# One pool for all eight PSUM banks, and every head group's output projection held to the step's end

## The chip, the cores and the metric

The kernel runs on one core of a Trainium2 chip. The metric is the device time of one execution in microseconds. A core has a matrix engine (TensorE; the profile calls its matmuls PE and its weight loads PEld), a vector engine (DVE), a scalar engine (ACT), a general engine (POOL) and a queue engine (SP) that here only issues transfers; 16 DMA engines move the data. TensorE writes its results to PSUM, which has eight banks of 2 KB for each of 128 partitions. Everything else is kept in SBUF.

## The reference

The input has 2048 tokens of 640 features. Four blocks follow one another: attention A, mixer B, attention A, mixer B, with the same weights in both layers. Attention runs over segments of 32 tokens, and every segment takes 8 memory rows from the output of the segment before it:

```python
for s in range(n_seg):                       # 64 segments of 32 tokens
    xs = x[:, s * seg_len:(s + 1) * seg_len, :]
    h = jnp.concatenate([mem, xs], axis=1)   # 8 + 32 rows
    q = jnp.einsum('btd,dhe->bhte', h, Wq)   # 32 heads of 192, D = 640
    k = jnp.einsum('btd,dhe->bhte', h, Wk)
    v = jnp.einsum('btd,dhe->bhte', h, Wv)
    p = softmax(where(mask, q @ k^T * scale, -1e9))
    o = p @ v
    o = jnp.einsum('bhte,hed->btd', o, Wo)
    mem = o[:, :M, :]
    outs.append(o[:, M:, :])
...
# mixer: h = gelu(layernorm(x) @ w1); four quarters shifted along the tokens; x1 = x + h @ w2
#        out = x1 + gelu(layernorm(x1) @ w3) @ w4
```

So a segment can't begin before the output projection of all 32 heads of the segment before it is known. Wq, Wk, Wv and Wo have 7.9 MB each in bf16, and don't fit into SBUF together.

## The kernel before

**Steps and lanes.** The two layers run as two lanes, the second `LAG` = 5 segments behind the first. There are 69 attention steps. In 59 of them both lanes are present, and a matmul then carries 80 columns: per lane 32 tokens and 8 memory rows. Every second step a mixer chunk of 64 tokens per lane begins. Its pieces are spread over the next one to two steps: w1 and w2 in the first step (the "heavy" one below, since the vector work of the mixer stands there as well), w3 over the boundary, w4 in the second ("light") step.

**A step.** The 32 heads are taken in 8 groups of 4 (`g` = 0 to 7). For each group the kernel runs the projections k, q and v (tiles `psk`, `psq`, `psv`: 30 matmuls each, 5 row blocks of the weights by 6), turns v over (`psvt`), then scores (`pss`), softmax in place, the transposed probabilities (`pst`), and the product with v (`pso`), which DVE copies to one of the `oT` tiles in SBUF. Then follows the output projection of the group: 30 matmuls (`f8` in `attention_step`, L653), 6 row blocks of Wo by 5, added up over all 8 groups in two PSUM tiles `psy`. After group 7, ACT copies the memory columns of `psy` into the next step's input (`fm`, L691), and DVE copies the rest for the mixer (`fy`, L699). `psy` is held from the first output matmul of the step until these copies.

**Weights.** SBUF keeps three of the five row blocks of every group of Wk, Wq and Wv, and two (group 0) or four (others) of six of Wo (`CUT`). The rest is loaded again in every step: 48 blocks of 192 KB for k, q, v and 18 blocks of 160 KB for Wo (four for group 0, two for each other group). They go through a ring of 16 slots (`wst`), of which the attention may hold 14 (`RING_A`). SP issues these loads in one queue ("wa"), sorted by due time; a load waits until its slot was read. The mixer's weights use up to five slots and are issued by POOL.

**The order.** `Plan` lists all operations with an engine, a duration and a due time, and `place()` simulates the engines: it takes the operation that can start first, and among those that can start within 0.03 us on TensorE the one with the earliest due time. An operation that needs a PSUM tile can only start when its pool has a free bank and its class is under its limit. The order found is written out; each engine then works through its list in order. `STEP` = 48 is the planned length of a step, `sl` = 6 that of a group.

**Banks.** `PSUM_BANKS` names the pools and `PSUM_USES` gives each class of tile its pool and its limit. The classes are y (the two `psy`), P (projections and `psvt`), S (`pss`, `pst`, `pso`) and B (everything of the mixer). Before, y has two banks of its own, and P, S and B share six, with limits of 4, 3 and 2.

**When an output projection runs.** This is set by `held`, which depends on the number of `oT` tiles:

```python
held = g >= NG - OT_BUFS + 1
at = base + STEP - HOLD + 0.5 * g if held else s0 + 1.9 * sl
ws = [block(t, "o", g, c, at + 0.03 * c) for c in range(GC)]
due = base + STEP - 1 + 0.02 * g if held else s0 + 2.0 * sl
```

With `OT_BUFS` = 7 the groups 2 to 7 are held: their matmuls are due at 47 us of the step, and their Wo blocks at 45 us and later. Groups 0 and 1 have their matmuls due at 12 and 18 us and their blocks at 11.4 and 17.4 us. A first operation on `psy` needs both of its banks at once.

Of the kernel before, what the change touches and what calls it, by code (L numbers as in the profile page):

```python
# [33 lines left out]
W4 = (1.5, 0.025)  # L34
W1 = (0.15, 0.04)
W2 = (0.4, 0.04)
PSUM_BANKS = {"y": 2, "x": 6}
PSUM_USES = {"y": ("y", 2), "P": ("x", 4), "S": ("x", 3), "B": ("x", 2)}
OT_BUFS = 7
V_BUFS = 2  # L40
VT_BUFS = 1
LAT = 0.2
# [43 lines left out]
class Plan:  # L86
# [11 lines left out]
    def add(self, e, d, due, fn, r=(), w=(), a=(), dma=0, queue=None, after=()):  # L98
        op = Op()
        op.e, op.d, op.due, op.fn, op.dma = e, d, due, fn, dma  # L100
        op.succ, op.ready, op.n = [], 0.0, 0
        op.i = len(self.ops)
        preds = set(after)
        slots = []
        for b in r:
            preds.update(b.writers)
        for b in w:
            preds.update(b.writers)
            preds.update(b.readers)
        for b in a:  # L110
            preds.update(b.base)
            preds.update(b.readers)
        for b in r:
            b.readers.append(op)
        for b in w:
            b.base = [op]
            b.writers = [op]
            b.readers = []
        for b in a:
            b.writers.append(op)  # L120
        for b in {id(b): b for b in (*r, *w, *a)}.values():
            if isinstance(b, Slotted):
                b.left += 1
                slots.append(b)
        op.slots = slots
        preds.discard(op)
        for p in preds:
            p.succ.append(op)
            op.n += 1
        self.ops.append(op)  # L130
        if queue is not None:
            self.queues.setdefault(queue, []).append(op)
        return op
# [117 lines left out]
def kernel(  # L251
# [59 lines left out]
    def ctile(shape, dtype, name):  # L311
        return const.tile(shape, dtype, name=name)
# [40 lines left out]
    vTs = [ctile([P, GC, NS], bf16, f"vTs{i}") for i in range(VT_BUFS)]  # L353
    oT = [ctile([P, GC, NS], bf16, f"oT{i}") for i in range(OT_BUFS)]
    sm = [ctile([P, 16], f32, f"sm{i}") for i in range(4)]
# [28 lines left out]
    def B(*key):  # L384
        if key not in bufs:
            bufs[key] = Buf()
        return bufs[key]

    plan = Plan({**PSUM_BANKS, "r": RING}, {**PSUM_USES, "ra": ("r", RING_A), "rb": ("r", RING_B)})
    add = plan.add  # L390
# [9 lines left out]
    def T(b):  # L400
        if b.obj is None:
            b.obj = b.make()
        return b.obj

    def mm_us(n, m=128, k=1):
        return k * (max(min(64, m), n) / 2400.0 + 0.0025)

    def dve_us(n, ps_=True):
        return ((120 if ps_ else 58) + n) / 960.0 + 0.02
# [80 lines left out]
    def attention_step(t):  # L490
# [84 lines left out]
        def attend(g):  # L575
# [60 lines left out]
            add("PE", mm_us(N, k=8), hi - 3, f6, r=(B("PT"), B("V", G % V_BUFS)), w=(pso,))  # L636
            o_ = oT[G % OT_BUFS]

            def f7(op):
                nc.vector.tensor_copy(out=o_[:, :, 0:N], in_=T(pso)[:, :, 0:N])  # L640
            add("DVE", dve_us(GC * N), hi - 4, f7, r=(pso,), w=(B("oT", G % OT_BUFS),))
            held = g >= NG - OT_BUFS + 1
            at = base + STEP - HOLD + 0.5 * g if held else s0 + 1.9 * sl
# [12 lines left out]
            if g < NG - 1:  # L656
                for c in range(GC):
                    def f8(op, c=c):
                        out_rows(0, YA, c, c + 1, 0)()
                        out_rows(YA, KC, c, c + 1, 1)()  # L660
                    add("PE", mm_us(N, k=KC), due, f8,
                        r=(ws[c][0], B("oT", G % OT_BUFS)), a=tuple(psy))
            else:
                for j, (m0, m1) in enumerate(((0, YA), (YA, KC))):
                    def f8(op, j=j, m0=m0, m1=m1):
                        out_rows(m0, m1, 0, GC, j)()
                    add("PE", mm_us(N, k=GC * (m1 - m0)), due + 0.5 * j, f8,
                        r=(*{id(b): b for b, _ in ws}.values(), B("oT", G % OT_BUFS)), a=(psy[j],))

# [499 lines left out]
```

## Time and profile before

| | |
|---|---|
| median of 8 runs | 3554.04 us (3544.17 to 3566.47) |
| profiled execution: time | 3555.9 us |
| profiled execution: span | 3554.0 us |
| PE busy / PEld busy | 3391.3 us (95%) / 3255.3 us (92%) |
| DVE, ACT, POOL busy | 67%, 48%, 25% |
| granted TensorE clock, mean | 0.992 |
| moved by DMA | 1094.80 MB, 308 GB/s over the span |
| PE matmuls / instructions | 84693 / 194567 |

The busy time of PE is modelled, since matmuls overlap; where matmuls follow one another without a pause the row of PE is full. A row of the timeline gives its start, its length, the engine and line, output and inputs, the number of instructions merged and, in brackets, the idle time just before it with what ended it. A table of windows gives busy time per engine for each stretch, the granted clock, the busy share of the DMA engines and GB/s.

### The profile page before, as it was taken

How to read it: one execution, taken by the hardware profiler on the slowest of the kernel's cores; microseconds unless marked ns; L12 is line 12 of the kernel's file. 1: busy time of each engine (PE TensorE's matmuls, PEld its weight loads, DVE VectorE, ACT ScalarE, POOL GpSimd, SP SyncE). 2: the span in 40 equal slices, each digit the busy share in tenths (PEclk: the TensorE clock that was granted, in tenths of full speed). 3: DMA queues.
4: the chain of work that ended last, by engine and by line, in shares of the span. 5: the costliest groups of instructions: out<-in, count | busy, mean ns of one | idle time of the engine just before them, and what ended most of it. 6: DMA issues, size and time to landing. Idle time of an engine off the chain costs nothing. (4 is left out here: it accounts for less than half of the span.)

```text
span 3554.0 us, 194567 instructions
## 1 busy us (share of the span) xinstructions
PE 3391.3 (95%) x84693; PEld 3255.3 (92%) x84693; DVE 2376.6 (67%) x7184; ACT 1709.2 (48%) x3583; POOL 882.1 (25%) x1581
## 2 busy tenths in 40 slices
PE   6989999999999999999999999999999999999997
PEld 4879999999999999999999999999999999999885
DVE  2556777677666767776676777776667777766555
ACT  2334455445454544454555555454545554544433
POOL 1122222222222222222222222222222222222222
PEclk9999999999999999999999999999999999999998
DMA  9999999999999999999999999999999999999997
GB/s 341 317 311 306 313 310 304 301 307 313 304 304 312 314 308 298 307 314 310 307 315 311 310 301 314 310 315 299 317 303 316 309 301 309 316 310 309 308 311 238
DMA packets 739865, 1094.80 MB, mean 308 GB/s; under 512 B 95870, under 2 KB 696204, under 8 KB 739008
## 3 DMA queue, kind: packets, MB, share of 16 engines
q1 hardware_dynamic: 674112, 879.77, 75.2%
q0 software_dynamic: 64896, 202.59, 17.1%
q8 instruction: 662, 10.85, 1.3%
q14 instruction: 195, 1.60, 0.1%
HBM read 1076.73 MB, written 5.24 MB: 304 GB/s over the span
## 5 line engine op out<-in xcount | busy, mean ns | idle before, releaser
L472 POOL DMA_DIRECT2D wst<-in_B_w_dram x1088 | 595.5, 548 | 1733.1 <-PE pss L586 284.1
L514 PEld LDWEIGHTS <-wst 128*128 128x128 bf16 x13248 | 555.0, 100 | 37.7 <-issue 13.7
L640 DVE CAST oT<-pso 128x480 bf16<-128x480 f32 (+1 forms) x552 | 340.6, 617 | 308.0 <-PE pso L634 306.2
L571 ACT COPY V<-psvt 80x768 bf16<-80x768 bf16 (+1 forms) x552 | 438.6, 795 | 224.3 <-PE psvt L567 221.2
L522 ACT CAST qT<-psq 128x480 bf16<-128x480 f32 (+1 forms) x552 | 292.7, 530 | 513.2 <-PE psq L514 512.7
L653 PE MATMUL psy<-oT,wo 128*128 128x80 bf16 (+1 forms) x10350 | 510.3, 199 | 11.8 <-DMA wo<-in_A_Wo_dram 5.2
L514 PE MATMUL psk<-hT,wk 128*128 128x80 bf16 (+1 forms) x9936 | 481.2, 199 | 11.7 <-issue 5.7
L514 PE MATMUL psq<-hT,wq 128*128 128x80 bf16 (+1 forms) x9936 | 474.2, 199 | 12.8 <-DMA wq<-in_A_Wq_dram 7.9
L597 DVE CUSTOM_DVE_ANT_1 pss<-pss,mask 80x320 f32<-80x320 f32 (+1 forms) x512 | 245.7, 480 | 323.0 <-PE pss L586 317.1
L555 PE MATMUL psv<-hT,wv 128*128 128x80 bf16 (+1 forms) x9936 | 453.0, 199 | 5.5 <-DMA wv<-in_A_Wv_dram 3.7
L561 ACT CAST vTs<-psv 128x480 bf16<-128x480 f32 (+1 forms) x552 | 292.4, 530 | 331.3 <-PE psv L555 322.7
L653 PEld LDWEIGHTS <-wo 128*128 128x128 bf16 x10350 | 423.2, 99 | 20.1 <-issue 7.8
L514 PEld LDWEIGHTS <-wq 128*128 128x128 bf16 x9936 | 407.1, 99 | 27.3 <-DMA wq<-in_A_Wq_dram 8.8
L514 PEld LDWEIGHTS <-wk 128*128 128x128 bf16 x9936 | 409.0, 99 | 21.6 <-issue 8.4
L555 PEld LDWEIGHTS <-wv 128*128 128x128 bf16 x9936 | 391.1, 100 | 15.3 <-DMA wv<-in_A_Wv_dram 5.0
L514 PE MATMUL psk<-hT,wst 128*128 128x80 bf16 (+1 forms) x6624 | 356.0, 199 | 15.8 <-DMA wst<-in_A_Wk_dram 8.3
L624 ACT COPY PT<-pst 80x320 bf16<-80x320 bf16 (+1 forms) x552 | 222.2, 403 | 293.4 <-PE pst L619 290.6
L555 PE MATMUL psv<-hT,wst 128*128 128x80 bf16 (+1 forms) x6624 | 350.5, 199 | 11.0 <-DMA wst<-in_A_Wv_dram 7.2
L609 DVE TENSOR_REDUCE sm<-pss 80x4 f32<-80x320 f32 (+1 forms) x552 | 252.5, 457 | 156.4 <-ACT pss L604 156.2
L514 PE MATMUL psq<-hT,wst 128*128 128x80 bf16 (+1 forms) x6624 | 334.5, 199 | 7.4 <-issue 4.5
L653 PE MATMUL psy<-oT,wst 128*128 128x80 bf16 (+1 forms) x6210 | 338.3, 199 | 1.0 <-DMA wst<-in_A_Wo_dram 0.7
L604 ACT ACTIVATE pss<-pss,sm 80x320 f32<-80x320 f32 (+1 forms) x552 | 262.0, 475 | 138.2 <-DVE sm L597 138.0
(132 smaller groups left out, 5482.5 us busy)
## 6 DMA issues: line engine op xcount, KB each, us to landing
wst<-in_A_Wk_dram SPq DMA_DIRECT2D x1104, 192.0 KB, 4.6
wst<-in_A_Wq_dram SPq DMA_DIRECT2D x1104, 192.0 KB, 4.9
wst<-in_A_Wv_dram SPq DMA_DIRECT2D x1104, 192.0 KB, 4.7
wst<-in_A_Wo_dram SPq DMA_DIRECT2D x1242, 160.0 KB, 4.5
wst<-in_B_w_dram POOLq DMA_DIRECT2D x748, 160.0 KB, 5.2
wst<-in_B_w_dram POOLq DMA_DIRECT2D x340, 192.0 KB, 5.1
wk<-in_A_Wk_dram SPq DMA_DIRECT2D x8, 576.0 KB, 7.3
wq<-in_A_Wq_dram SPq DMA_DIRECT2D x8, 576.0 KB, 7.6
```

What stands on the lines that cost most here:

```text
L472: return (nc.sync if B_SP else nc.gpsimd).dma_start(out=T(b)[:, 0:wd], in_=src)
L514: nc.tensor.matmul(out=o[:, c, 0:N], lhsT=w[:, c * P:(c + 1) * P], rhs=h[:, kc, c0:c0 + N], start=pq.begin(), stop=True, skip_group_check= ...
L522: nc.scalar.copy(out=q[:, :, 0:N], in_=T(pq)[:, :, 0:N])
L555: nc.tensor.matmul(out=o[:, c, 0:N], lhsT=w[:, c * P:(c + 1) * P], rhs=h[:, kc, c0:c0 + N], start=pv.begin(), stop=True, skip_group_check= ...
L561: nc.scalar.copy(out=vs[:, :, 0:N], in_=T(pv)[:, :, 0:N])
L571: nc.scalar.copy(out=V_[0:N, :, 0:Dh], in_=T(pt)[0:N].rearrange("n c f -> n (c f)").rearrange("n (i e) -> n i e", i=HG))
L597: nc.vector.tensor_tensor_reduce(out=o, in0=o, in1=maskt.unsqueeze(1).to_broadcast([N, HG, N]), scale=-scale, scalar=3.0e38, op0=ALU.add, ...
L604: nc.scalar.activation(out=o, in_=o, func=ACT.Exp, bias=sm_[0:N, 0:1], scale=-1.0)
L609: nc.vector.reduce_sum(out=sm_[0:N, 4:4 + HG], in_=o, axis=AX.X)
L624: nc.scalar.copy(out=Pt[0:N, :, 0:N], in_=T(pst)[0:N, :, 0:N])
L640: nc.vector.tensor_copy(out=o_[:, :, 0:N], in_=T(pso)[:, :, 0:N])
L653: nc.tensor.matmul(out=T(psy[j])[:, m - m0, c0:c0 + N], lhsT=w[:, m * P:(m + 1) * P], rhs=o_[:, c, 0:N], start=psy[j].begin(), stop=True, ...
```

## The change

```diff
-PSUM_BANKS = {"y": 2, "x": 6}
-PSUM_USES = {"y": ("y", 2), "P": ("x", 4), "S": ("x", 3), "B": ("x", 2)}
-OT_BUFS = 7
+PSUM_BANKS = {"x": 8}
+PSUM_USES = {"y": ("x", 2), "P": ("x", 4), "S": ("x", 4), "B": ("x", 4)}
+OT_BUFS = 9
```

All four classes draw from one pool of eight banks. The limits of S and B rise to four each; those of P (4) and y (2) stay. With `OT_BUFS` = 9, `held` is `g >= 0`, so it holds for every group: the output projections of groups 0 and 1 become due at 47.00 and 47.02 us of the step in place of 12 and 18, and their six streamed Wo blocks at 44.06 to 44.65 us in place of 11.4 to 17.6. Two more `oT` tiles of 960 bytes per partition are kept in SBUF. The sets of matmuls, copies and transfers are the same as before; what changes is the order that `place()` writes out, and the bank and `oT` tile that each operation uses.

## The prediction

> **What bounds the kernel now.** I read the busy shares first, then stretches of the span, then one step's boundary in the timeline, then the waits of PE and of SP's queue.
>
> ```profile
> PE 3391.3 (95%) x84693; PEld 3255.3 (92%) x84693; DVE 2376.6 (67%) x7184; ACT 1709.2 (48%) x3583; POOL 882.1 (25%) x1581
> ...
> q1 hardware_dynamic: 674112, 879.77, 75.2%
> q0 software_dynamic: 64896, 202.59, 17.1%
> ```
>
> PE is full, and the DMA engines nearly are: the two queues of data take 92.3%. In five long stretches from 388 to 3012 us PE's busy time misses 14.5, 15.0, 9.7, 10.6 and 11.3 us, together 61 us of 2624, or 2.3%. So better cover can give only about 2%. Next, how the gaps lie within a heavy step (1754 to 1804 us) and at the end of the light step ahead of it:
>
> ```profile
> 1735.00:1745.00 10.00, 10.00 (x243) 9.60 (x241) 7.66 (x23) 4.51 (x9) 4.54 (x8) 1.00 1.00 341
> 1745.00:1754.00 9.00, 8.86 (x233) 8.70 (x230) 3.87 (x10) 3.82 (x10) 1.14 (x2) 1.00 0.82 255
> 1754.00:1764.00 10.00, 10.00 (x258) 9.73 (x255) 8.22 (x26) 4.61 (x10) 2.28 (x3) 1.00 0.94 302
> 1764.00:1774.00 10.00, 9.38 (x228) 9.06 (x226) 8.00 (x25) 6.18 (x15) 2.74 (x5) 1.00 0.89 292
> 1774.00:1784.00 10.00, 10.00 (x245) 9.62 (x242) 9.02 (x30) 4.91 (x10) 2.70 (x6) 1.00 0.96 318
> ```
>
> The columns are busy us of PE, PEld, DVE, ACT and POOL, the clock, the DMA share and GB/s. The end of the step (second row) is already full on PE, and there DVE has little to do (3.87 of 9 us) and the DMA engines drop to 0.82. In the first 30 us of the heavy step DVE is busy 8.0 to 9.0 of 10 us, and there PE has a hole, in front of a transposition of probabilities:
>
> ```profile
> 1772.54 0.35 PE L619 MATMUL pst<-ident,Pm 80*80 80x80 bf16 x4 [0.62 <-DVE Pm L611]
> 1772.71 0.39 PE L514 MATMUL psq<-hT,wq 128*128 128x80 bf16 x6
> 1773.10 0.52 PE L653 MATMUL psy<-oT,wo 128*128 128x80 bf16 x10
> 1773.45 0.46 PE L634 MATMUL pso<-PT,V 80*128 80x80 bf16 x8
> 1773.74 0.53 PE L653 MATMUL psy<-oT,wo 128*128 128x80 bf16 x10
> 1774.10 0.52 PE L653 MATMUL psy<-oT,wst 128*128 128x80 bf16 x10
> ```
>
> The matmuls after it are the output projection of group 1: work that needs nothing from DVE just then, where DVE is late. Last, SP's queue around the boundary at 1754.24 us:
>
> ```profile
> 1742.18 5.60 SPq L448 DMA_DIRECT2D wst<-in_A_Wo_dram  x8
> 1748.15 1.55 SPq L448 DMA_DIRECT2D wst<-in_A_Wk_dram  x2
> 1749.79 2.52 SPq L448 DMA_DIRECT2D wst<-in_A_Wq_dram  x2
> 1752.40 0.86 SPq L448 DMA_DIRECT2D wst<-in_A_Wv_dram  x2
> ...
> SPq L448 <- PE psy L653: 394.1, 500, 3.4
> ```
>
> The last line is SP's longest wait: a load waits for a ring slot that output matmuls have yet to read. The next step's Wv blocks are issued by 1753.3 us and used from 1758.1 us, 4.8 us later; the page gives 4.7 us as the median to landing. The Wq blocks are issued by 1752.3 us and used at 1755.95 and 1756.17 us, against a median of 4.9. The lead over PE is at its thinnest at the start of a step.
>
> **The change, part by part.**
>
> *Moved matmuls.* Two groups by 30 matmuls. Thirty follow one another in 1.07 us (the q projection starts at 1755.31, the k projection ahead of it at 1754.24), so 2.15 us of PE work per step go from the first 20 us to the end. The work itself costs the same. What it covered and what it will cover decide.
>
> *At the end of the step* it covers nothing that isn't covered: PE is full there. Worth 0. The chain that sets the end (scores of group 7 at 1746.66, `pst` at 1750.43, `pso` at 1751.48, first matmul of group 7's output at 1753.14, copy at 1753.99) gets 2.15 us more to hide behind; it had enough.
>
> *In the light step* DVE is below 80% in the first 20 us (5.14 and 7.68 of 10 us, 1705 to 1725) and PE is full; nothing waits for the cover that leaves. 0.
>
> *In the heavy step* DVE has 25.2 us of work in the first 30 us. With 2.15 us of PE's work gone the same work stands against 27.85 us: 84% become 91%. From below this costs 0, since the planner may put resident Wo blocks back into a hole, if both `psy` banks are free. From above it costs all 2.15 us of each of about 30 heavy steps, 65 us. The nearest row is the 0.62 us hole above. I take half of one more such hole, 0.31 us by 30: **+9 us**; half, because what is put back fills about as many holes as it leaves.
>
> *Moved transfers.* Six Wo blocks per step are issued late. In SP's order the four of group 0 and two of group 1 now come ahead of those of groups 2 and 3 and of group 7's v blocks: ten blocks instead of four stand in front of the latter. Of 14 slots up to ten then hold Wo blocks whose matmuls have the latest due time of the step. The loads for groups 5, 6 and 7 wait for the matmuls of groups 0 and 1; before, they waited for projections long done. Behind them in the same queue stand Wk, Wq and Wv of the next step. The slot for its first block is the one of group 2's first streamed block, before and after. But its distance to the boundary shrinks: before, between this block's matmuls (1746.48) and the boundary stood 1.88 us of attention work of groups 6 and 7 (0.29 + 0.22 + 0.59 + 0.34 + 0.15 + 0.29 us by the starts in the timeline). Some of it will now run in between group 0's and 1's matmuls, ahead of group 2's. From above all 1.88 us, in 59 two-lane steps 111 us; from below 0, if the attention work stays where it was. `pst` and `pso` of group 7 can't move ahead, as they end a chain of 5 us, so I take half, about 1.0 us, of later issue. A block that lands 1.0 us late costs PE less: before the streamed blocks of k are needed, resident blocks of q and v (18 matmuls, 0.64 us each) can be run. Half again: 0.5 us by 59: **+30 us**. The Wo blocks no longer asked for at 11 to 18 us relieve the DMA engines there; PE is full in this place, so 0.
>
> *More banks for P, S and B.* In mid-step they may hold eight, not six. What PE waited for a bank is next to nothing: in the waits I find 0.7 us (`psv` behind `psq`) and 0.6 us (`psq` behind the copy of `psvt`), but the order was made so that no bank is waited for, so a shortage shows as order. It does show at the end: the scores of group 7 start when the copy of group 6's `pst` ends (1746.47 + 0.42 us against 1746.66), though their keys and queries were ready by about 1746. The bounds: no gain, or all of the holes before `pst` (17.9 us in the waits of PE) and all waits of the mixer's last product for its weights (14.1 us). I take half of the first, **-9 us**: with a fourth S tile a softmax can begin earlier, but its length on DVE stays.
>
> *First step, tail, `oT` tiles.* The first step runs at 342 GB/s with the DMA engines full until its copy at 97.9 us; the same bytes are loaded in another order: 0, at most the 1.5 us of its longest hole either way. The tail after 3517 us is the mixer's alone: 0. Two more `oT` tiles take no time.
>
> Sum: 9 + 30 - 9 = +30 us on the profiled execution's 3555.9 us, 3586 us. That execution lies 1.9 us above the median of the runs, so the forecast is **3584 us**, 0.8% slower.
>
> One rule speaks the other way. The Trainium skill's "Perfetto Trace Analysis", section "Matmul Optimizations", says that all eight banks should be put to use, and section "Optimization Strategy" that a gap which repeats can mean that there isn't enough PSUM for the next tile. By this rule the 61 us of holes are the gain to be had, and the sum without the other terms would be about 3493 us. The trace does not agree: the holes here end on DVE, on a transfer or on "issue", and hardly any on the release of a bank.
>
> **The rivals.**
>
> *More banks smooth the step.* One mechanism: S and B at four let scores, softmax and mixer start earlier in the heavy step, so that `Pm` is there when PE comes to `pst`. It decides if the next step's blocks don't come later than now. For it: DVE waits 350 us in all for `pss`, so scores could come earlier. Against it: DVE at 80 to 90% in this place. Price: the 17.9 us before `pst` and part of the 14.1 us before the mixer's `y`: about -20 us, **3534 us**.
>
> *It doesn't do what it says.* The planner fills any hole over 0.03 us with a resident Wo block of group 0 or 1 as soon as two banks are free, takes `psy` in mid-step, and P, S and B have six banks as before. For it: 30 of a step's 48 Wo blocks are resident, so that filler is always at hand. Against it: the light step has no hole. **3554 us**, within 0.2%.
>
> *A jam.* `psy` needs two banks at once; where DVE is late, P with four and S with four can hold all eight, and the filler is missing when it is wanted; at the end the ring stands still until `psy` starts, and the transfers at 92% have no room to catch up. One more hole like SP's longest wait on `psy` (3.4 us) in every heavy step: 30 by 3.4 = 102 us, **3656 us**. For it: the DMA share of 0.82 at the end says that transfers already idle there. Against it: at about 1745 us I count three P, two S and one B tile in use, which leaves two.
>
> **How the numbers follow.** Forecast 0.45, gain 0.31, no change 0.09, jam 0.15. A measurement of this kernel can tell about 0.2%, 7 us, from no change. Faster 0.31, same 0.09, slower 0.60. The range that holds 8 in 10 goes from 3526 us (28 of the 32 us of holes that the banks could close at most, 17.9 + 14.1) to 3670 us (the jam with a little over it); the forecast's own range is 3562 to 3620 us.
>
> **What would show it.** Right: L653's first matmuls at more than 30 us into a step, later issue of the next step's Wk, Wq and Wv, larger waits of `psk`, `psq`, `psv` on `wst` in the first 5 us of a step (now PE idles 0.2 us there, summed over 58 steps of the timeline), and more before `pst` in heavy steps. SP's wait on `psy` grows beyond 394 us. Wrong: pairs of steps at 99 to 100 us in place of 100.9 (29 pairs from 388.57 to 3314.67 us), `pst`'s wait gone, and no new wait at the boundary; or `psy` matmuls still at 10 to 20 us.

## The result, and the profile after

| | before | after |
|---|---|---|
| median | 3553.95 us (32 runs) | 3536.68 us (11 runs, 3525.32 to 3541.76) |
| ratio, 95% interval | | 0.9947 (0.9936 to 0.9959) |
| span of the profiled execution | 3554.0 us | 3535.0 us |
| mean pair of steps, 29 pairs | 100.90 us | 100.02 us |
| mean granted TensorE clock | 0.992 | 0.988 |

The change made the kernel 0.5% faster, 17 us, where 30 us more were forecast. (The two medians by themselves give a ratio of 0.9951, inside the interval.) A pair of steps is taken from the copy of the memory columns (L691) at the end of a step to the one two steps later; for the kernel after the stretch goes from 392.40 to 3293.09 us.

The 29 pairs together became 25 us shorter (2926.10 to 2900.69 us), more than the whole span (19 us): what lies ahead of the pairs and behind them became 6 us longer (627.9 to 634.3 us). The lower mean clock belongs to these two ends as well: within the pairs the granted clock is 1.00 in both kernels, ahead of them 0.98 before and 0.97 after, behind them 0.91 and 0.89.

The page of the kernel after, busy us by engine and the two queues of data:

```profile
PE 3383.0 (96%) x84693; PEld 3255.3 (92%) x84693; DVE 2377.0 (67%) x7184; ACT 1714.4 (48%) x3583; POOL 880.3 (25%) x1581
...
q1 hardware_dynamic: 674112, 879.77, 75.6%
q0 software_dynamic: 64896, 202.59, 17.1%
```

The row to read is PEld. Its busy time is the same to a tenth as before (3255.3 us), so the span less PEld is an account of the difference: 298.7 us of idle weight loads before, 279.7 after, a difference of 19.0 us, which is the whole difference of the spans. That the two busy times agree to a tenth is chance: when the kernel after was run once more it had 3257.5 us of busy weight loads and 276.2 us of idle ones in a span of 3533.7 us, so the account is good to a few us. The idle time of a single line is less sure: L555, the v projections, had 32.0 us in the one execution and 40.5 in the other. PE's own busy time is a worse account: it fell by 8.3 us for the same matmuls, as its rows overlap and hide short pauses. The Trainium skill's "Trainium Kernel Development and Optimization", section "Performance Expectations", says that for the distance of a kernel from its limit the busy share of weight loads is a good measure and busy time of matmuls a bad one, because matmuls are pipelined; this case agrees, with 19.0 of 19.0 us in the one row and 10.7 us of idle (3554.0 - 3391.3 = 162.7 against 3535.0 - 3383.0 = 152.0) in the other.

Where the 19 us come from is read in the groups of weight loads: line, shape, count, busy us, mean ns, then the idle time just before the group and what ended it. First the kernel before:

```profile
L514 PEld LDWEIGHTS <-wst 128*128 128x128 bf16 x13248 | 555.0, 100 | 37.7 <-issue 13.7 <-DMA wst<-in_A_Wk_dram 12.1 <-DMA wst<-in_A_Wq_dram 4.4
...
L653 PEld LDWEIGHTS <-wst 128*128 128x128 bf16 x6210 | 264.6, 99 | 4.4 <-DMA wst<-in_A_Wo_dram 1.6 <-issue 0.2
...
L619 PEld LDWEIGHTS <-Pm 80*80 80x80 bf16 (+1 forms) x2208 | 124.8, 116 | 27.9 <-DVE Pm L611 24.1 <-issue 0.8
```

and the same groups of the kernel after:

```profile
L514 PEld LDWEIGHTS <-wst 128*128 128x128 bf16 x13248 | 554.9, 100 | 29.6 <-issue 9.3 <-DMA wst<-in_A_Wq_dram 6.8 <-DMA wst<-in_A_Wk_dram 1.9
...
L653 PEld LDWEIGHTS <-wst 128*128 128x128 bf16 x6210 | 270.0, 100 | 19.9 <-DMA wst<-in_A_Wo_dram 12.8 <-issue 4.6
...
L619 PEld LDWEIGHTS <-Pm 80*80 80x80 bf16 (+1 forms) x2208 | 127.5, 116 | 9.4 <-DVE Pm L611 2.2 <-issue 1.6 <-DVE kT L537 0.7
```

Three things move. The idle time before the transposition of probabilities (L619) falls from 27.9 to 9.4 us; that before all k and q projections (L514, three groups) from 86.6 to 68.1; that before the output projections (L653, two groups) rises from 24.5 to 45.7. So a gain of about 37 us has 21 us taken off it again; the other lines make up the rest. The waits of PE, and SP's wait on the output matmuls, kernel after:

```profile
PE psy L653 <- DMA wst<-in_A_Wo_dram: 8.9, 13, 1.5
...
PE psy L653 <- DVE oT L640: 3.2, 6, 1.9
...
PE pst L619 <- DVE Pm L611: 0.6, 2, 0.5
...
SPq L448 <- PE psy L653: 243.2, 473, 2.0
```

PE's wait before `pst` is all but gone (17.9 us before); a wait for Wo blocks has come (0.7 us before). SP waits less on `psy`, not more (394.1 us before). The heavy step from 1745.06 to 1794.32 us of the kernel after, in windows with the same columns as in the prediction:

```profile
1745.00:1755.00 10.00, 10.00 (x264) 9.78 (x261) 8.03 (x25) 4.43 (x10) 2.28 (x3) 1.00 0.96 314
1755.00:1765.00 10.00, 10.00 (x256) 10.00 (x252) 8.37 (x25) 7.02 (x17) 2.74 (x5) 1.00 0.97 323
1765.00:1775.00 10.00, 10.00 (x243) 9.63 (x241) 9.09 (x31) 5.82 (x12) 2.37 (x5) 1.00 0.89 290
...
1789.00:1794.00 5.00, 4.88 (x133) 4.78 (x130) 2.67 (x6) 1.60 (x3) 0.00 (x0) 1.00 0.89 286
```

At the same distance from the start of the step the kernel before has 8.22, 8.00 and 9.02 us of DVE (1754 to 1784 us). So DVE is about as busy as before (25.5 against 25.2 of 30 us), and the hole in its second row, where PE had 9.38 of 10 us, is gone. A small one stands in the last five microseconds of the step, at the output projections.

### The profile page after: what moved, and what is told of

It is laid out like the page before. It is cut to its first block, busy times and chain, and to the rows that moved or that the text cites. A ratio compares the mean times of both kernels' runs of the same rounds, so it can differ in the third digit from the quotient of the medians.

```text
span 3535.0 us, 194719 instructions
## 1 busy us (share of the span) xinstructions
PE 3383.0 (96%) x84693; PEld 3255.3 (92%) x84693; DVE 2377.0 (67%) x7184; ACT 1714.4 (48%) x3583; POOL 880.3 (25%) x1581
## 5 line engine op out<-in xcount | busy, mean ns | idle before, releaser
L571 ACT COPY V<-psvt 80x768 bf16<-80x768 bf16 (+1 forms) x552 | 439.2, 796 | 333.6 <-PE psvt L567 323.9
L514 PEld LDWEIGHTS <-wst 128*128 128x128 bf16 x13248 | 554.9, 100 | 29.6 <-issue 9.3
L653 PE MATMUL psy<-oT,wo 128*128 128x80 bf16 (+1 forms) x10350 | 510.4, 199 | 19.0 <-DMA wo<-in_A_Wo_dram 7.7
L555 PE MATMUL psv<-hT,wv 128*128 128x80 bf16 (+1 forms) x9936 | 476.9, 199 | 7.0 <-issue 4.0
L514 PE MATMUL psk<-hT,wk 128*128 128x80 bf16 (+1 forms) x9936 | 462.8, 199 | 7.2 <-issue 6.5
L514 PE MATMUL psq<-hT,wq 128*128 128x80 bf16 (+1 forms) x9936 | 455.0, 199 | 13.5 <-DMA wq<-in_A_Wq_dram 7.2
L653 PEld LDWEIGHTS <-wo 128*128 128x128 bf16 x10350 | 423.3, 99 | 25.8 <-issue 11.1
L555 PEld LDWEIGHTS <-wv 128*128 128x128 bf16 x9936 | 404.5, 99 | 21.1 <-issue 5.1
L514 PEld LDWEIGHTS <-wq 128*128 128x128 bf16 x9936 | 393.8, 100 | 21.8 <-DMA wq<-in_A_Wq_dram 8.2
L514 PEld LDWEIGHTS <-wk 128*128 128x128 bf16 x9936 | 398.2, 99 | 16.7 <-issue 9.5
L653 PE MATMUL psy<-oT,wst 128*128 128x80 bf16 (+1 forms) x6210 | 352.4, 199 | 12.2 <-DMA wst<-in_A_Wo_dram 8.9
L514 PE MATMUL psk<-hT,wst 128*128 128x80 bf16 (+1 forms) x6624 | 352.8, 199 | 9.1 <-issue 7.8
L555 PE MATMUL psv<-hT,wst 128*128 128x80 bf16 (+1 forms) x6624 | 341.9, 199 | 7.1 <-DMA wst<-in_A_Wv_dram 3.8
L514 PE MATMUL psq<-hT,wst 128*128 128x80 bf16 (+1 forms) x6624 | 327.0, 199 | 6.3 <-DMA wst<-in_A_Wq_dram 4.1
```

The source lines that it names most:

```text
L514: nc.tensor.matmul(out=o[:, c, 0:N], lhsT=w[:, c * P:(c + 1) * P], rhs=h[:, kc, c0:c0 + N], start=pq.begin(), stop=True, skip_group_check= ...
L555: nc.tensor.matmul(out=o[:, c, 0:N], lhsT=w[:, c * P:(c + 1) * P], rhs=h[:, kc, c0:c0 + N], start=pv.begin(), stop=True, skip_group_check= ...
L571: nc.scalar.copy(out=V_[0:N, :, 0:Dh], in_=T(pt)[0:N].rearrange("n c f -> n (c f)").rearrange("n (i e) -> n i e", i=HG))
L653: nc.tensor.matmul(out=T(psy[j])[:, m - m0, c0:c0 + N], lhsT=w[:, m * P:(m + 1) * P], rhs=o_[:, c, 0:N], start=psy[j].begin(), stop=True, ...
```

## The experiments

All ratios are to the kernel before on the same chip, with 95% intervals. The kernel before ran between 3554.67 and 3566.56 us (medians) on the chips used. Every kernel computes the whole of the reference. The idle times given are sums over the groups of weight loads of a line, as above. The diffs are against the kernel after where nothing else is said.

### First: the two edits apart

**The banks alone.**

```diff
-OT_BUFS = 9
+OT_BUFS = 7
```

> The banks alone: one pool of eight and the limits of four, but OT_BUFS = 7, so groups 0 and 1 keep their early output projection. Theory A (the gain comes from more banks for P, S and B, whatever the outputs do): ratio to the kernel before about 0.995, and PE's wait on Pm before pst goes from 17.9 us to under 5. Theory B (banks in mid-step are only there when psy lets go of them, so both edits are needed): psy takes two of the eight from about 11 us of each step, P, S and B have six as before; ratio 0.998 to 1.003, wait on Pm stays at 10 us or more. Theory C (holding alone is the gain): ratio 1.000.

Measured: 0.9982 (0.9968 to 0.9995). The wait on `Pm` is gone, but a wait on a bank stands in its place in every heavy step; 29 times, 18.4 us in all. In the waits and in the timeline of this kernel:

```profile
PE psq L514 <- ACT V L571: 18.4, 29, 0.7
```
```profile
1766.12 0.45 PE L634 MATMUL pso<-PT,V 80*128 80x80 bf16 x8
1767.20 0.59 PE L514 MATMUL psq<-hT,wq 128*128 128x80 bf16 x12 [0.63 <-ACT V L571]
1767.62 0.88 PE L653 MATMUL psy<-oT,wo 128*128 128x80 bf16 x20
```

A q projection reads nothing that the copy `V` (L571) writes; it waits for the bank that this copy empties. With `psy` taking two of the eight from 11 us of the step, the others run short in the place where PE waited before. Theory B has the time right, and in the place of the wait that it named stands this one.

**The hold alone.**

```diff
-PSUM_BANKS = {"x": 8}
-PSUM_USES = {"y": ("x", 2), "P": ("x", 4), "S": ("x", 4), "B": ("x", 4)}
+PSUM_BANKS = {"y": 2, "x": 6}
+PSUM_USES = {"y": ("y", 2), "P": ("x", 4), "S": ("x", 3), "B": ("x", 2)}
```

> The hold alone: OT_BUFS = 9, banks as before (two for psy, six for P, S, B with limits 4, 3, 2). Theory A and my recorded terms (cover lost in the heavy step +9 us, ring lead lost +30 us): 1.003 to 1.011, SP's wait on psy above 394 us, wait on Pm above 17.9 us. Theory B: no bank is won in mid-step, so 0.999 to 1.003, wait on Pm about as before. Theory C (moving PE-only work away from the heavy step's vector work changes the order so that pst no longer waits): 0.995, wait on Pm under 5 us.

Measured: 0.9979 (0.9966 to 0.9992). The idle time before `pst` falls to 7.6 us without one more bank, that at L514 to 67.5; that at L653 rises to 56.3 us. None of the three theories foresaw this mixture. The cost stands at the end of the step, where PE waits for Wo blocks (10.0 us in all, 0.7 before) and for group 7's `oT` (13.4 us, 1.8 before), most of it 0.39 us in every second step from 641 to 3154 us:

```profile
1847.87 0.53 PE L653 MATMUL psy<-oT,wst 128*128 128x80 bf16 x10
1848.78 0.59 PE L653 MATMUL psy<-oT,wo 128*128 128x80 bf16 x12 [0.39 <-DVE oT L640]
```

**The pool and the hold, with the limits of before.**

```diff
-PSUM_USES = {"y": ("x", 2), "P": ("x", 4), "S": ("x", 4), "B": ("x", 4)}
+PSUM_USES = {"y": ("x", 2), "P": ("x", 4), "S": ("x", 3), "B": ("x", 2)}
```

> One pool of eight and the hold, but the limits of before: S 3, B 2. Theory A in the form that the total counts (8 instead of 6 in mid-step): 0.995 to 0.997, as P 4 + S 3 + B 2 = 9 already exceed 6. Theory A in the form that the limits count (a fourth S tile lets a softmax begin earlier): 0.999 to 1.002, with the wait on Pm back above 10 us.

Measured: 0.9941 (0.9927 to 0.9956), as with the limits of four. The limits do nothing that can be measured; the shared pool does.

**The hold and the limits of four, `psy` with banks of its own.**

```diff
-PSUM_BANKS = {"x": 8}
-PSUM_USES = {"y": ("x", 2), "P": ("x", 4), "S": ("x", 4), "B": ("x", 4)}
+PSUM_BANKS = {"y": 2, "x": 6}
+PSUM_USES = {"y": ("y", 2), "P": ("x", 4), "S": ("x", 4), "B": ("x", 4)}
```

> The hold and the limits of four, but psy with two banks of its own and six for the rest, as before. If banks in mid-step are the gain (A or B): 0.999 to 1.004, as P, S and B share six again, and with higher limits one class can crowd out another. If the hold or the limits are the gain: 0.995.

Measured: 0.9978 (0.9967 to 0.9990), as the hold alone, and between the two forecasts. So, with all groups held, sharing the pool takes 0.9979 to 0.9947 (on one chip, with the limits of before, 0.9979 to 0.9941).

### Second: number of banks, transfers, and the scatter of orders

**Seven banks in the pool.**

```diff
-PSUM_BANKS = {"x": 8}
-PSUM_USES = {"y": ("x", 2), "P": ("x", 4), "S": ("x", 4), "B": ("x", 4)}
+PSUM_BANKS = {"x": 7}
+PSUM_USES = {"y": ("x", 2), "P": ("x", 4), "S": ("x", 3), "B": ("x", 2)}
```

> Hold, limits of before, one pool of only seven banks, so that P, S and B have at most seven in mid-step instead of eight. If the number of banks in mid-step is what the second part of the gain comes from (hold alone 0.9979, with eight banks 0.9941): in between, 0.995 to 0.997. If the gain is sharing with psy as such: as with eight, 0.994. If it is luck of one particular order: anywhere, above 0.998 too.

Measured: 0.9955 (0.9939 to 0.9970). It lies between, as the number of banks would have it, though its interval overlaps those with six and with eight.

**Wo blocks due 4 us earlier.**

```diff
-HOLD = 4.0
+HOLD = 8.0
```

> The changed kernel with HOLD = 8: the Wo blocks are due 4 us earlier in SP's queue, nothing else. If the late issue of Wo blocks costs time at the end of the step (PE's weight loads idle 45.7 us at L653 now, 24.5 us before): faster, 0.992 to 0.994, L653's idle under 35 us. If the blocks then hold ring slots that projections need: slower, 0.997 to 1.003, with more waits of psk, psq, psv on wst. If neither matters: 0.9947.

Measured: 1.0465 (1.0446 to 1.0483), outside all three forecasts. In most steps SP's queue now puts sixteen Wo blocks ahead of group 6's v blocks and all eighteen ahead of group 7's; in the kernel after it is none and ten. In the waits of PE:

```profile
PE psy L653 <- DVE oT L640: 66.9, 96, 1.5
PE psv L555 <- DMA wst<-in_A_Wv_dram: 54.1, 71, 2.0
```

PE waits for the v blocks, and then for an `oT` at the end of the chain that begins with them. That Wo blocks hold up the blocks behind them in the queue, as the prediction had it under "moved transfers", is seen here; but the v blocks of the same step pay for it, where the prediction put the price on the next step.

**Another order, after and before.** The planner's tie margin on TensorE changes, nothing else; the first against the kernel after, the second against the kernel before.

```diff
-LOOK = 0.03
+LOOK = 0.04
```

> The changed kernel with the planner's tie margin on TensorE at 0.04 us in place of 0.03: another order with the same banks and the same hold. If the gain is of the edits: 0.993 to 0.997. If it is luck of one order, orders scatter by as much as the gain and this may land above 0.998.

> The kernel before with the planner's tie margin at 0.04 us: the scatter of orders without the edits. If the gain is of the edits: 0.998 to 1.003. If a new order alone can do it: 0.995 to 0.997.

Measured: 0.9937 (0.9922 to 0.9952) and 1.0000 (0.9986 to 1.0014). In one other order of each kernel the difference is about the same, so it isn't the luck of one order. In the second kernel the idle time before `pst` stays, 29.2 us.

### Third: where in the step, and in the queue

**Eight `oT` tiles:** group 0 early, 1 to 7 held, one pool.

```diff
-OT_BUFS = 9
+OT_BUFS = 8
```

> The changed kernel with eight oT tiles: groups 1 to 7 are held, group 0 keeps its output projection at 12 us of the step, so psy takes its two banks there. If the second part of the gain is the banks that psy leaves free until the end (theory B): only six for P, S and B from about 11 us on, 0.996 to 0.999. If it is the number of matmuls that move: about half of the gain, 0.997. If only the limits or the single pool count: 0.9947. A wait of PE on the release of a bank, as with the banks alone (psq on the copy of psvt, 17.7 us), would speak for theory B.

Measured: 0.9918 (0.9893 to 0.9942). That is a lower ratio than with all groups held (0.9947, and 0.9938 when it was run again), though the intervals overlap, and though the bank wait of the first experiment is back (18.3 us, 29 times). It lies below all that theory B named, which ends theory B as the account of the gain. The idle time at L653 is 23.6 us, as in the kernel before: the cost there comes with group 0.

**Wo blocks due 2 us and 1 us later.**

```diff
-HOLD = 4.0
+HOLD = 2.0
```

> The changed kernel with HOLD = 2: the Wo blocks are due 2 us later, behind group 7's v blocks and closer to the next step's. If what is left of L653's idle (45.7 us against 24.5 before) is Wo blocks that come late: slower, 1.000 to 1.010, L653's idle above 60 us. If ring slots held by Wo blocks are what costs, as with HOLD = 8 (1.0465): faster, 0.991 to 0.994, with less wait of psv on wst.

```diff
-HOLD = 4.0
+HOLD = 3.0
```

> The changed kernel with HOLD = 3, one us later: the same question with half the step. If HOLD = 4 lies at the best place for this kernel too: 0.994 to 0.998. If the best place moved when six more blocks came into the burst: 0.991 to 0.993.

Measured: 0.9998 (0.9982 to 1.0014) and 1.0026 (1.0010 to 1.0043); L653's idle time is 72.7 and 72.4 us, and PE's wait for Wo blocks there 26.8 and 31.3 us (8.9 with `HOLD` = 4). The first is what was forecast for blocks that come late; the second was in neither forecast. The burst of Wo blocks has no slack on this side: one microsecond later loses the gain. Four earlier makes the kernel 4.7% slower than before; nothing between was tried, and each of these is one order.

**The kernel before with `HOLD` = 8** (same line of the diff as for the kernel after).

> The kernel before with HOLD = 8: the same 4 us of earlier due time for its twelve late Wo blocks. If it is the hold of all groups that makes the queue sensitive (18 blocks against 14 ring slots, all waiting for the matmuls with the latest due time): about 1.000 to 1.010, far below the 1.0465 of the changed kernel. If any Wo burst placed that early stops the v blocks of group 7: 1.03 to 1.05.

Measured: 1.0465 (1.0442 to 1.0489), the same as with the change and in the range of the second forecast. So it isn't the hold of all groups that makes the queue sensitive. Here ten Wo blocks stand ahead of group 6's v blocks and all twelve ahead of group 7's. Ten ahead of group 7's alone, as in the kernel after, cost nothing like it.

### Fourth: group 0 and group 1 apart

**Group 1 moved alone:** eight `oT` tiles and the banks of before, so against the kernel before one line.

```diff
-OT_BUFS = 7
+OT_BUFS = 8
```

> Eight oT tiles (groups 1 to 7 held, group 0 at 12 us) with the banks of the kernel before: group 1's move alone. If its move alone takes the wait on Pm away: L619's idle about 9 us, not 27.9, and 0.994 to 0.997 with L653's idle near 24 us. If the pool is needed for it: 0.999 to 1.001.

Measured: 0.9911 (0.9890 to 0.9932), better than either forecast. The kernel in which only group 1's thirty matmuls and two transfers move is 0.9% faster, without a bank; no other order of it was run. It doesn't close the hole before `pst`, as its groups of weight loads show:

```profile
L653 PEld LDWEIGHTS <-wst 128*128 128x128 bf16 x6210 | 266.2, 99 | 4.2 <-DMA wst<-in_A_Wo_dram 1.2 <-issue 0.3
...
L514 PEld LDWEIGHTS <-wst 128*128 128x128 bf16 x13248 | 555.6, 100 | 27.7 <-DMA wst<-in_A_Wk_dram 9.5 <-issue 5.6 <-DMA wst<-in_A_Wq_dram 5.2
...
L619 PEld LDWEIGHTS <-Pm 80*80 80x80 bf16 (+1 forms) x2208 | 124.9, 116 | 31.0 <-DVE Pm L611 25.6 <-issue 1.8 <-DVE kT L537 0.5
```

L619 keeps 31.0 us; L514 falls from 86.6 to 67.5 us over its three groups, L653 to 19.8.

**Group 0 at 24 us of the step, the others held, one pool.**

```diff
-            held = g >= NG - OT_BUFS + 1
-            at = base + STEP - HOLD + 0.5 * g if held else s0 + 1.9 * sl
+            held = g >= 1
+            at = base + STEP - HOLD + 0.5 * g if held else s0 + 3.9 * sl
...
-            due = base + STEP - 1 + 0.02 * g if held else s0 + 2.0 * sl
+            due = base + STEP - 1 + 0.02 * g if held else s0 + 4.0 * sl
```

> The changed kernel with group 0's output projection due at 24 us of the step (its blocks at 23.4), the others held. psy then takes its banks after the place in the heavy step where PE waited. If the hole there is a matter of banks: PE's wait of psq on the copy of psvt (17.6 us with eight oT tiles) is gone. If the cost at L653 is group 0's four streamed blocks in the burst: L653's idle about 24 us, not 45.7. Both together: 0.986 to 0.990. If both are luck: 0.992 to 0.995.

Measured: 0.9916 (0.9895 to 0.9938). The bank wait is gone, L653's idle time is 23.5 us, both as expected of their causes, but the sum fell short: a new wait for mixer weights at L1022 (8.9 us) came.

**The same with the banks of before:** the three lines above, and `PSUM_BANKS` and `PSUM_USES` as in the kernel before.

> The same with the banks of the kernel before. If the single pool is worth 12 us by itself (0.9979 to 0.9941 with all groups held): about 0.990 to 0.993. If the pool only mends what the last burst does to the end of the step: the same as with the single pool, 0.986 to 0.990.

Measured: 0.9886 (0.9864 to 0.9908), 3519.75 us. This is in the range named for a pool that only mends what the last burst does. With the burst small again no gain of the single pool can be measured: the two intervals overlap, and the kernel without it has the lower median. The hole before `pst` is closed here with six banks for P, S and B (L619 10.1 us).

**The kernel after once more**, unchanged, on this chip.

> The changed kernel as it is, on the chip of these runs: 0.9937 to 0.9959 again. Against it the three others are to be read.

Measured: 0.9938 (0.9918 to 0.9958).

**Group 0 held, groups 1 and 2 at 24 and 30 us,** with the banks of before: a burst of 14 streamed blocks, group 0's four among them.

```diff
-            held = g >= NG - OT_BUFS + 1
-            at = base + STEP - HOLD + 0.5 * g if held else s0 + 1.9 * sl
+            held = g not in (1, 2)
+            at = base + STEP - HOLD + 0.5 * g if held else s0 + 2.9 * sl
...
-            due = base + STEP - 1 + 0.02 * g if held else s0 + 2.0 * sl
+            due = base + STEP - 1 + 0.02 * g if held else s0 + 3.0 * sl
```

> Banks of before, nine oT tiles, group 0 held and groups 1 and 2 at 24 and 30 us: 14 streamed Wo blocks in the last burst, as with e17 and e18, but group 0's four among them. If the size of the burst decides: L653's idle 20 to 30 us, and 0.987 to 0.993. If group 0's blocks at the head of the burst decide: L653's idle 45 us or more, and 0.996 to 1.000.

In this expectation e17 is group 0 at 24 us with the banks of before, and e18 group 1 moved alone. Measured: 0.9911 (0.9894 to 0.9929), the range named for the size of the burst. L653's idle time is 34.7 us, in neither range: nearer to the other bursts of 14 blocks (19.8 to 25.6 us) than to those of 18 with these banks (52.2 and 56.3). So the size of the burst decides more of it than which group is in it. The rest may be group 0's four blocks at its head, or the output matmuls of groups 1 and 2 in mid-step; that wasn't tried apart.

**The best version with another order:** group 0 at 24 us, banks of before, `LOOK` = 0.04.

> e17 (banks of before, group 0 at 24 us, the others held) with the planner's tie margin at 0.04 us: another order. If its gain is of the placement: 0.986 to 0.991. If it is one lucky order: 0.992 or more.

Measured: 0.9887 (0.9866 to 0.9908), 3513.36 us. Both orders agree; this version beats the kernel before and the kernel after.

## Why the prediction was wrong

The table builds the change up piece by piece. The third column is the step's ratio times 3555 us; the runs come from several chips, and an interval is about 0.2% or 7 us either way. The last column is how much the 29 pairs of two-lane steps of the profiled execution became shorter or longer.

| built up | ratio | this step | in the 29 pairs |
|---|---|---|---|
| before | 1 | | |
| group 1 held | 0.9911 | -32 us | -18 us |
| group 0 held too | 0.9979 | +24 us | +6 us |
| one pool, limits of four | 0.9947 | -11 us | -13 us |

A large part of the first two steps lies ahead of the pairs and behind them. There a change of order alone moves as much: with `LOOK` = 0.04 the time outside the pairs fell by 8 us in the kernel before and by 14 us in the version with group 0 at 24 us, while the pairs changed by 3 and 6 us. So what a placement is worth is read from the pairs; that the whole 32 us of the first step are group 1's is not shown.

**What bounds the kernel: right.** What was won and lost stands as idle time of PE's weight loads, and no version gained more than 1.1%, where the holes allowed about 2%.

**"In the heavy step [...] I take half of one more such hole, 0.31 us by 30: +9 us": this step failed, in its sign.** It took DVE's 25.2 us of work in the first 30 us of a heavy step as given, let PE's work in this place shrink by 2.15 us, and so had DVE's share rise from 84 to 91% and the hole before `pst` grow. The runs show the opposite. Averaged over the 29 heavy steps of the pairs, the weight loads idle 1.98 us in the first 30 us before and 1.13 us after: 25 us less in all, where 9 us more were forecast. The hold does this without the pool (1.05 us); with group 1 alone it is 1.73 us. And DVE's share didn't rise: in these 30 us it is busy 24.9 us before and 25.0 after, as the place of the output matmuls was filled with other matmuls.

Nor was DVE's share a limit near at hand. The prediction's own last window has DVE busy 9.02 of 10 us with the row of PE full, and elsewhere in the kernel before DVE is busy 4.86 of 5 us while the weight loads don't pause:

```profile
2990.50:2995.50 5.00, 5.00 (x136) 5.00 (x133) 4.86 (x16) 3.43 (x7) 1.81 (x3) 1.00 0.98 328
```

The hole itself belongs to group 0: it stays when group 1 alone moves (31.0 us at L619), closes when group 0 leaves the first 20 us as well (7.6, 10.1, 9.0 us with six banks for the others), and turns into a wait for a bank when `psy` starts early within one pool. What in the new order lets `Pm` come in time wasn't tried apart. Nor was which side of group 1's move brings its 18 us in the pairs, the matmuls or the two transfers that go with them; 11 us of them are idle time before k and q projections, for a part of which the profile names no releaser ("issue").

**"Moved transfers [...] +30 us": for the hold alone the size was near, by luck; the place was not.** The term was a price at the next step's k, q and v. SP's queue around a boundary of the kernel after (copy at 1794.32 us):

```profile
1782.80 6.31 SPq L448 DMA_DIRECT2D wst<-in_A_Wo_dram  x8
1789.21 0.86 SPq L448 DMA_DIRECT2D wst<-in_A_Wk_dram  x2
1790.16 1.22 SPq L448 DMA_DIRECT2D wst<-in_A_Wq_dram  x2
1791.47 1.86 SPq L448 DMA_DIRECT2D wst<-in_A_Wv_dram  x2
```

Averaged over 56 steps, the next step's first Wk block is issued 5.0 us ahead of the copy (5.5 before), the first Wq block 3.7 us (3.9) and the first Wv block 2.5 us (2.7): later, as forecast, but by 0.1 to 0.5 us in place of 1.0. PE idles 0.8 us in the first 5 us of the steps, summed over 58 of them (0.2 us before), where 0.5 us in every step were forecast. The price is paid ahead of the boundary, within the burst, where PE waits for Wo blocks and, with separate banks, for group 7's `oT`. In the last 10 us of a step the weight loads idle 0.18 us on average before, 0.13 with group 1 alone, 0.67 with the hold alone and 0.33 after: over 58 steps 29 us more for the hold alone, and 9 us more with the pool. It is group 0 that has four streamed blocks, and with them the last burst has 18, against 14 slots of the ring. That the number of slots decides is argued and not shown, since the ring wasn't changed.

**"More banks for P, S and B [...] -9 us": near in size, by luck, for another reason.** The pool is worth 11 us with all groups held, but neither by a fourth S tile (the limits do nothing) nor by the hole before `pst` (which the hold closes without it). It takes away a part of what the burst costs: L653's idle time falls with it from 56.3 to 39.3 us with the limits of before, and from 52.2 to 45.7 with limits of four. With a smaller burst no gain of it can be measured. The rule that I weighed, to use all eight banks (the Trainium skill, "Perfetto Trace Analysis", section "Matmul Optimizations"), doesn't say how to divide them: the kernels before and after both use eight. The one run with seven (0.9955) can't be told from the same kernel with eight (0.9941). For the division, 0.9886 with two and six and 0.9916 with all eight shared are no clear difference either.

**"At the end of the step [...] Worth 0", "In the light step [...] 0", "First step, tail [...] 0":** the first is wrong by what the burst costs there. For the second no run stands alone; the light steps of the pairs became 0.24 us longer (49.50 to 49.74 us), 7 us in all, and the heavy ones 1.12 us shorter (51.40 to 50.28 us). The 6 us more outside the pairs are within what another order does there.

**The signs.** What the prediction named as signs of being wrong came: pairs of 100.02 us, and `pst`'s wait gone. L653's first matmuls went where it said: in two-lane steps they start from 37 us on in a light step and from 31 us on in a heavy one.

**The rivals.** "More banks smooth the step" named 3534 us, and 3536.68 were measured. That its number was right is luck, since its mechanism was not: it had the 17.9 us before `pst` closed by banks. The hold alone closes that hole, and the banks alone put another wait of 18.4 us in its place. It got 0.31 and not more because I had priced the hold as a loss of 39 us without a row that showed what fills a place that comes free. The case that `psy` starts early all the same is out, by the first matmuls of L653. No jam showed; SP's longest wait on `psy` fell from 3.4 to 2.0 us.

## What to carry to other kernels

In this kernel work that needs no other engine did best where the other engines have little to do. Such work is no cover for a late engine if an order made by a planner has other work to put in its place, and a busy share of 84% on that engine doesn't say that it is near its limit: look in the same profile for a stretch with a higher share. When work moves, its transfers move with it: look at the size of the burst that they join, at what stands behind it in the queue and at the slots of the ring, and move the part with few transfers first. Undo a change piece by piece even where it wins: with group 0 left out of the last burst, and without the single pool, the gain is about twice as large (0.9886 against 0.9938 on one chip). And split a difference by stretches of the span: a change meant for the repeating steps may show at the ends, where another order does as much.

## What the runs showed of the hardware that was not expected

Weight loads overlap matmuls, and their idle time kept an account of the span that was good to a few us (19.0 of 19.0 us here), while the matmul row hid nearly half of it. DVE was busy 4.86 of 5 us in the kernel before, and 4.74 of 5 us (1760 to 1765 us) in the kernel after, without a pause in the weight loads. And one queue of transfers, with the DMA engines at 92 to 93% of the span, left a due time no slack on the late side: `HOLD` = 4 gave 0.9947, one microsecond later 1.0026; four earlier gave 1.0465.
